# Earlier x sums, a table of Sinkhorn steps and a finer dealing of the last block's L2 in an attention and mixture-of-experts kernel

## The chip, the cores and the metric

The kernel runs on one core of a Trainium2 chip. The metric is the device time of one execution in microseconds (us); the kernel before takes 978.73 us, the median of 6 runs from 977.86 to 979.73.

The core's engines are called as the profile calls them: PE (TensorE, matmuls; PEld is its loading of weights), DVE (VectorE), ACT (ScalarE), POOL (GpSimd) and SP (SyncE, which here only issues DMAs). Each engine takes its own instructions in their order, and semaphores hold an instruction back until what it needs is done.

## The reference

A linear attention with a cosine weighting of the positions makes `x`, and a mixture of 8 experts is applied to all tokens, each expert weighted by a table `P` that Sinkhorn's iteration makes of the gate's logits. The shapes: q, k, v are (8, 8, 576, 64); x is (4608, 512); w1 is (8, 512, 1024), w2 (8, 1024, 512).

```python
k_p, q_p = phi(k, cos_w, sin_w), phi(q, cos_w, sin_w)     # relu, times cos and sin
kv = np.einsum('bhsf,bhsd->bhfd', k_p, v)
z = np.sum(k_p, axis=2)
num = np.einsum('bhsf,bhfd->bhsd', q_p, kv)
den = np.einsum('bhsf,bhf->bhs', q_p, z)[..., None] + 1e-06
x = (num / den)                                           # laid out as tokens x 512
logits = x @ w_gate
P = np.exp(logits - logits.max())
for _ in range(8):
    P /= P.sum(1, keepdims=True) + 1e-09
    P /= P.sum(0, keepdims=True) + 1e-09
    P *= N / E
for e in range(E):
    h = np.maximum(x @ w1[e], 0.0)
    out += P[:, e:e + 1] * (h @ w2[e])
```

## The kernel before

**Two stages.** In the first, blocks 0 to 6, the attention of batch b + 1 is made beside expert 0's two layers of the block of 512 tokens before it. A block has 16 slots (`NS = 2 * FT`): eight for the first layer (`ffn1`, one 128-row slice of the hidden dimension with four matmuls each, then a Relu on ACT into `hT`), eight for the second (`ffn2`, half of a token tile's product over the hidden dimension each, then a copy into `acc`). What the attention does in a slot is written out by hand with `at(block, slot, fn, ...)`. `x`, transposed, lies in one tile `xT`.

In the second stage, blocks 7 and 8 of expert 0 follow (the loop `for j in range(B - 1, NJ)`), then experts 1 to 7 (the loop `for e in range(1, E)`). These multiply 2 x 2 blocks with seven products in place of eight (a Strassen-like scheme), and so need sums of the operands:

- The tokens of an expert are six units (`NU`) of 768 tokens: 384 of the first half of the tokens, 384 of the second. `x_sums(n, ts)` makes unit n's sums S1, S2 and S4 and overwrites a part of `xT`, with four operations of 128 x 768 on DVE, and SP stores the three sums in `x_saved` in DRAM. For later experts `x_again` loads them.
- `w1_steps` gives the four operations that make the sums of one slice of w1 (T2, T3, T4, one in place).
- `group` makes one of four slices of the first layer of a unit: seven products of two matmuls of 384 columns into three PSUM banks X (`h_ps`), Y (`copied_ps`) and Z (`p7_ps` in the program, `p_ps` in the profile). ACT copies X to Y and takes two snapshots u2 and u4 of X, which DVE adds to Z with a clamp (L885). After each product `group` calls `fill()`, seven times in all, in which other work is put between the products. The last product of a group, with its add-and-clamp, is put off (`late`) into the next group.
- `Pair` makes the second layer of two token tiles with seven products P1 to P7 of four matmuls of 256 columns. P1 is copied by ACT into a bank W (L990), and the sums of H that the pair needs are made on DVE (L970); each result is multiplied by a column of `P_tok` and added to `acc` on DVE (L955).

**What the fills hold.** For expert 1's unit 0 the fill is `start_fill`: parts of block 8's second layer, dealt by the generator `dealt` (four parts of two matmuls for each of four token tiles), and steps of Sinkhorn's iteration. From then on it is `pair_fill`: of every four fills three take the next step of the pairs' stream once its place in the stream is due (`slot2`), so that a unit's 28 fills take 21 steps, which are three pairs. `pair_fill` also gates the tiles of `acc` that expert 0 wrote, that is, multiplies them by their column of `P_tok` (`gate`, L1107), as `P_tok` was not known before.

**Sinkhorn's iteration** is the generator `sinkhorn`, with five steps an iteration: (1) row sums and their reciprocal, (2) the table times these, and partial column sums `colp`, (3) up to two of the w1 operations that `tw_steps` holds for the iteration, (4) a matmul of `ones_all` with `colp`, which sums over the partitions, and the remaining w1 operations, (5) a reciprocal and the table times this. `balanced(n)` takes n steps. Eight iterations are 40 steps. The kernel before takes three at slot 1 of block 7, then from slot 5 on one and four in two slots of every five, 23 by the end of block 8, and one in most fills of expert 1's unit 0.

**Order.** While `te`, `ve` and `se` are the wrappers of class `InOrder` (`bound`), the instructions of PE, DVE and ACT stand exactly as written. DVE's is taken away after expert 1's unit 0, ACT's from expert 2 on; the scheduler may then place an instruction as early as its operands allow. Four of the last gatings are so placed in the time of expert 1's first two units.

**Buffers.** The pools of the first stage (`p1`), with `kp_pool` (four buffers `k_p`) and the ones for q and its transposes among them, are closed before the second stage, and its tiles (weights of expert 1, `H`, S1 to S4, T and V) take their place in SBUF, so a write there waits for the last use of what lay there. `H` has two halves that the units take in turn; block 7 writes the half that lies over the `k_p` buffers.

Of the kernel before, what the change touches and what calls it, by code (L numbers as in the profile page):

```python
# [11 lines left out]
F16 = mybir.dt.float16  # L12

AX = mybir.AxisListType
ALU = mybir.AluOpType
# [10 lines left out]
def kernel(  # L26
# [10 lines left out]
    nc = tc.nc  # L37
    P = nc.NUM_PARTITIONS

    B, H, S, D = q.shape  # L40
    E, Dm, F = moe_w1.shape
    N = B * S
# [112 lines left out]
    def ffn2(hT, w, c0, g, y_ps, fts):  # L155

        for ft in fts:
            te.matmul(
                out=y_ps,
                lhsT=hT[:, ft, c0 : c0 + P],  # L160
                rhs=w[1][:, ft, :],
                start=(ft == 0),
                stop=(ft == FT - 1),
            )
        if FT - 1 in fts:

            if g % 2 == 0 or g < (B - 1) * TCH // P:
                se.copy(out=acc(g), in_=y_ps)
            else:
                ve.tensor_copy(out=acc(g), in_=y_ps)  # L170

    def store(g, cols=slice(0, Dm), queues=(nc.sync, nc.sync)):
        for half, queue in enumerate(queues):
            w_ = 2 * g + half
            b, c = w_ // C, w_ % C
            rows = out[b * S : (b + 1) * S].rearrange("(p c) d -> p c d", c=C)
            queue.dma_start(
                out=rows[:, c, cols], in_=acc(g)[half * HP : (half + 1) * HP, cols]
            )

    with ExitStack() as p1:
        ld = p1.enter_context(tc.tile_pool(name="ld", bufs=4))
# [421 lines left out]
        def at(block, slot, fn, *args):  # L604
            todo.setdefault((block, slot), []).append((fn, args))
# [62 lines left out]
        for j in range(B):  # L668
# [82 lines left out]
            if j == 1:  # L751
                for name in "qkv":
                    for half in range(2):
                        at(j, 12, load, b + 2, half, name, True)
            elif j and b + 2 < B:
                for half in range(2):
                    at(j, 11 + half, load, b + 2, half, "qkv", True)
        y_pss = {}
        for j in range(B - 1):
            if j:  # L760
# [34 lines left out]

    NT = N // 2
    TU = 3 * P
    NU = NT // TU  # L800
    KH = KT // 2
    FH = FT // 2
    UG = TU // P
    DH = Dm // 2
    w_next = load_weights(wB, 1)

    H = hB.tile([P, 2, FT, 2 * TU], F16, name="H")
# [12 lines left out]
    Y = ps_k.tile([P, TCH], FP32, name="copied_ps")  # L820
    Z = ps_k.tile([P, TCH], FP32, name="p7_ps")

    def x_part(half, kh, n):
        t0 = half * NT + n * TU
        return xT[:, kh * KH : (kh + 1) * KH, t0 : t0 + TU]

    x_saved = dram.tile([NU, 3, P, KH * TU], F16, name="x_saved")

    def x_tiles():
        return [s2_pool.tile([P, KH, TU], F16, name=name) for name in ("S1", "S2", "S4")]  # L830

    def x_sums(n, ts):

        a11, a12, a21, a22 = (x_part(i, j, n) for i in range(2) for j in range(2))
        s1, s2, s4 = (t[:] for t in ts)
        for out_, in0, in1, op in (
            (s1, a21, a22, ALU.add), (s2, s1, a11, ALU.subtract),
            (s4, a12, s2, ALU.subtract), (a21, a11, a21, ALU.subtract),
        ):
            ve.tensor_tensor(out=out_, in0=in0, in1=in1, op=op)  # L840
            yield
        for i, t in enumerate(ts):
            nc.sync.dma_start(out=x_saved[n, i], in_=t[:].rearrange("p k t -> p (k t)"))

    def x_again(n, ts):
        for i, t in enumerate(ts):
# [8 lines left out]
    def w1_steps(w, i):  # L855

        cols = [slice((j * FH + i) * P, (j * FH + i + 1) * P) for j in range(2)]
        b11, b12 = (w[0][:, 0:KH, c] for c in cols)
        b21, b22 = (w[0][:, KH:KT, c] for c in cols)
        T2, T3, T4 = (t_pool.tile([P, KH, P], F16, name=f"T{k_}_{i}") for k_ in (2, 3, 4))  # L860

        def sub(out, in0, in1, op=ALU.subtract):
            return lambda: ve.tensor_tensor(out=out, in0=in0, in1=in1, op=op)

        steps = [
            sub(T3[:], b22, b12), sub(T2[:], T3[:], b11, ALU.add), sub(b12, b12, b11),
            sub(T4[:], b21, T2[:]),
        ]
        return (b11, b12, b21, b22, T2[:], T3[:], T4[:]), steps
# [216 lines left out]
    def balanced(steps):  # L1086
        for _ in range(steps):
            next(balance, None)

    def dealt(hT, w, tiles, parts):  # L1090

        for i, (c0, g) in enumerate(tiles):
            for part in range(parts):
                ffn2(
                    hT, w, c0, g, rows2[i % 3][:],
                    range(part * FT // parts, (part + 1) * FT // parts),
                )
                yield
# [16 lines left out]

    balance = sinkhorn()

    tws, tw_steps = [], [[] for _ in range(8)]
    for i in range(FH):
        tw, tw_steps[1 + i] = w1_steps(w_next, i)  # L1120
        tws.append(tw)
    xs_first = [x_tiles() for _ in range(2)]
    xs_next = xs_first[0]
    sums_x = x_sums(0, xs_next)
    for j in range(B - 1, NJ):
        hT = next_h()
        tiles = dealt(
            hT, w0, [(ts * P, j * TCH // P + ts) for ts in range(TCH // P)],
            2 if j < NJ - 1 else 4,
        )  # L1130
        for slot in range(NS):
            if slot < FT:
                ffn1(hT, w0, j, [slot])
            elif j < NJ - 1:
                next(tiles)
            else:
                break
            if j == B - 1 and slot == 0:
                gates(B - 1, Z[:])
            if j == B - 1 and slot:  # L1140
                next(sums_x, None)
            if j == NJ - 1:
                if slot == 0:
                    sums_x = x_sums(1, xs_first[1])
                next(sums_x, None)
            since = (j - B + 1) * NS + slot - 5
            if since == -4:
                balanced(3)
            elif since >= 0 and since % 5 < 2:
                balanced((1, 4)[since % 5])  # L1150


    OFFSETS = {"P1": 0, "P2": 3, "P7": 4, "P6": 5, "P4": 8, "P5": 9, "P3": 13}
# [1 line left out]
    OFFSETS_LAST = {"P1": 0, "P2": 3, "P7": 4, "P6": 7, "P5": 8, "P4": 9, "P3": 10}  # L1155
    stream = []
    final = []
    slot2 = -2
    n_pairs = 0

    def add_pairs(hT, e, w, n):
# [13 lines left out]
    def start_fill():  # L1175

        nonlocal k_fill
        if k_fill % 7 in (0, 2, 3, 5):
            next(tiles, None)
        if k_fill % 6 != 1:  # L1180
            balanced(1)
        k_fill += 1

    def pair_fill():
        nonlocal k_fill, slot2
        k_fill += 1
        if k_fill % 4 and stream and stream[0][0] <= slot2:
            _, pair, name = stream.pop(0)
            pair.step(name)
        if (k_fill % 7 == 6 or k_fill % 7 == 4 and k_fill % 4 in (1, 2)) and ungated:  # L1190

            gate(ungated.pop(0))
        slot2 += bool(k_fill % 4)

    mark(Y[:])
    for e in range(1, E):
        if e == 2:
            se = nc.scalar
        w = w_next
        for n in range(NU):  # L1200
            hT = next_h()
            xs = xs_next
            for i in range(FH):
                group(hT, tws[i], xs, n, i, start_fill if e == 1 and n == 0 else pair_fill)
                m = (n + 1) % NU
                if e == 1 and m:

                    if n == 0:
                        xs_next = xs_first[1]
                        continue  # L1210
                    if i == 0:
                        xs_next = x_tiles()
                        sums_x = x_sums(m, xs_next)
                    next(sums_x)
                    if i == FH - 1:
                        next(sums_x, None)
                elif i == 1:
                    xs_next = x_tiles()
                    if not (e == E - 1 and m == 0):
                        x_again(m, xs_next)  # L1220

                if e > 1 and n == 0 and i == 0:
                    tws[FH - 1] = w1_sums(w, FH - 1)
                if e + 1 < E and n == NU - 1:
                    if i:
                        tws[i - 1] = w1_sums(w_next, i - 1)
                    else:
                        w2_first(w_next)
            if e == 1 and n == 0:
                k_fill = 0  # L1230
                for _ in tiles:
                    pass
                for _ in balance:
                    pass
                mark(W2[:])
                w2_first(w)
                for _ in range(2):
                    gate(ungated.pop(0), nc.gpsimd)
                ve = nc.vector
            if n == 0 and e + 1 < E:  # L1240
                w_next = new_weights(wA if e % 2 else wB)
                load_w1(w_next, e + 1, 1)
            if n == 2 and e + 1 < E:
                load_w2(w_next, e + 1, 1)
            add_pairs(hT, e, w, n)
# [36 lines left out]
```

The softmax here doesn't subtract the row's maximum and nothing guards it: scores larger than these inputs give would overflow.

## Time and profile before

| what | us |
|---|---|
| median of 6 runs | 978.73 |
| the profiled execution | 979.73 |
| its span, first to last instruction | 978.0 |
| PE busy | 963.7 |
| DVE busy | 807.3 |
| ACT busy | 563.6 |
| block 6 | about 145 to 164 |
| blocks 7 and 8 | about 164 to 186 |
| expert 1, unit 0 (with block 8's second layer) | about 186 to 208 |
| one unit of a later expert | about 18.4 |
| last group's end to the end | about 961 to 978 |

A row of the timeline has the start, the time from the first start to the last end, the engine, the line and the operation, the tile written and the tiles read, the shape, and how many instructions are merged; in brackets is how long the engine had stood idle and what it then waited for. A line L109 is that of the wrapper `InOrder`, through which most operations go, so that groups are told apart by their tiles; buffer numbers are left out of names, so that `copied_ps` stands for both `copied_ps` and `copied2_ps`, the bank in which the column sums are made.

### The profile page before, as it was taken

What the parts mean: (1) busy time and instruction counts of PE and PEld (TensorE: products, weight loads), DVE (VectorE), ACT (ScalarE), POOL (GpSimd) and SP (SyncE); (2) the same over time, 40 slices, a digit from 0 to 9 for tenths busy, and PEclk for the clock granted to TensorE, in tenths of its full rate; (3) what the DMA queues carried; (4) which work ended last, traced back from release to release, by engine and by line L of the source; (5) the groups of instructions that cost most, each with busy time, mean ns of one, the idle gap of its engine ahead of it and who ended that gap; (6) DMA issues with size and microseconds to landing.
All of it is one profiled execution on the core that took longest, in us unless ns stands there. A gap on an engine that the chain in (4) does not pass through costs nothing.

```text
span 978.0 us, 20236 instructions
## 1 busy us (share of the span) xinstructions
PE 963.7 (99%) x7855; PEld 675.8 (69%) x7855; DVE 807.3 (83%) x1833; ACT 563.6 (58%) x1262; POOL 60.7 (6%) x82
## 2 busy tenths in 40 slices
PE   9999999999999999999999999999999999999997
PEld 6545555457777777777777777777777777777775
DVE  6766775888988888988888888988888888988887
ACT  5756665467776555555555555555555555555551
POOL 6231110010000000000000000000000000000001
PEclk9999999999999999999999999999999999999999
DMA  9999986330103401223103401323103401104435
GB/s 163 182 146 181 152 141 111 68 68 28 48 25 77 84 25 35 64 54 68 39 25 78 83 25 39 62 55 66 40 25 77 84 25 37 38 26 121 127 88 128
DMA packets 80336, 73.54 MB, mean 75 GB/s; under 512 B 33264, under 2 KB 72176, under 8 KB 80240
## 3 DMA queue, kind: packets, MB, share of 16 engines
q0 software_dynamic: 27232, 30.94, 20.3%
q1 hardware_dynamic: 52768, 41.06, 17.5%
q8 instruction: 61, 1.00, 0.4%
q14 instruction: 35, 0.29, 0.1%
q10 hardware_dynamic: 240, 0.26, 0.1%
HBM read 83.12 MB, written 12.98 MB: 98 GB/s over the span
## 4 chain that ended last, share of the span: by engine, by line
PE 89%; DMA 4%; DVE 3%; issue 2%; ACT 1%; POOL 1%; POOLq 0%; ACTq 0%; SPq 0%
PE rows_ps L109 33%; PE h_ps L109 27%; PE p_ps L109 11%; PE copied_ps L109 11%; PE y_ps L109 4%; PE small_ps L109 3%; DMA k_ld<-in_k_dram 1%; DMA w2e<-in_moe_w_dram 1%; DMA w1e<-in_moe_w_dram 1%; DVE P_tok L109 1%; DVE colp L109 0%; POOL q_ld L202 0%; DVE rs L109 0%; DVE acc_hi L955 0%; DVE rr L109 0%
## 5 line engine op out<-in xcount | busy, mean ns | idle before, releaser
L955 DVE SCALAR_TENSOR_TENSOR acc_lo<-rows_ps,P_tok,acc_lo 128x512 f32<-128x512 f32 (+1 forms) x322 | 203.1, 639 | 75.0 <-PE rows_ps L109 74.9
L109 PEld LDWEIGHTS <-H 128*128 128x128 f16 x2080 | 203.1, 98 | 82.5 <-issue 1.2
L891 ACT CAST u<-h_ps 128x384 f16<-128x384 f32 x288 | 137.6, 478 | 131.2 <-PE h_ps L109 131.2
L109 PEld LDWEIGHTS <-w1e 128*128 128x128 f16 x1632 | 157.7, 98 | 67.6 <-issue 5.2
L885 DVE CUSTOM_DVE_ANT_0 H<-p_ps,u 128x384 f16<-128x384 f32 x329 | 180.8, 550 | 6.6 <-PE p_ps L109 6.6
L109 PEld LDWEIGHTS <-hs 128*128 128x128 f16 x1500 | 146.6, 98 | 56.2
L109 PE MATMUL h_ps<-S,w1e 128*128 128x384 f16 x672 | 164.1, 326 | 0.7 <-ACT u L109 0.6
L109 PE MATMUL p_ps<-xT,T 128*128 128x384 f16 x672 | 164.1, 326 | 0.1
L109 PE MATMUL rows_ps<-V,H 128*128 128x256 f16 x1000 | 150.0, 273 | 0.7 <-DVE acc_hi L955 0.7
L109 PE MATMUL rows_ps<-w2e,hs 128*128 128x256 f16 x1000 | 150.0, 273 | 0.0
L109 PE MATMUL h_ps<-xT,w1e 128*128 128x384 f16 (+1 forms) x616 | 148.7, 350 | 0.1
L923 ACT ACTIVATE H<-h_ps 128x384 f16<-128x384 f32 x144 | 70.6, 490 | 95.1 <-PE h_ps L109 95.1
L109 PEld LDWEIGHTS <-T 128*128 128x128 f16 x1008 | 98.4, 98 | 30.1 <-issue 3.6
L109 PE MATMUL rows_ps<-w2e,H 128*128 128x256 f16 (+1 forms) x568 | 92.3, 285 | 0.0
L904 ACT COPY copied_ps<-h_ps 128x384 f32<-128x384 f32 x144 | 67.5, 469 | 35.5 <-PE h_ps L109 35.5
L914 ACT ACTIVATE H<-copied_ps 128x384 f16<-128x384 f32 x144 | 70.8, 492 | 20.4 <-PE copied_ps L109 20.4
L109 PE MATMUL h_ps<-S,T 128*128 128x384 f16 x336 | 81.8, 324 | 0.4 <-ACT copied_ps L109 0.3
L109 PE MATMUL copied_ps<-xT,w1e 128*128 128x384 f16 x336 | 82.1, 326 | 0.0
L109 PE MATMUL copied_ps<-w2e,H 128*128 128x256 f16 x504 | 75.5, 272 | 0.0
L109 PE MATMUL rows_ps<-V,hs 128*128 128x256 f16 x500 | 74.9, 272 | 0.0
L955 DVE SCALAR_TENSOR_TENSOR acc_lo<-copied_ps,P_tok,acc_lo 128x256 f32<-128x256 f32 x126 | 60.0, 476 | 0.6 <-PE copied_ps L109 0.2
L955 DVE SCALAR_TENSOR_TENSOR acc_hi<-rows_ps,P_tok,acc_hi 128x512 f32<-128x512 f32 (+1 forms) x56 | 41.3, 737 | 20.6 <-PE rows_ps L109 19.7
(145 smaller groups left out, 949.9 us busy)
## 6 DMA issues: line engine op xcount, KB each, us to landing
S<-x_saved SPq DMA_DIRECT2D x108, 192.0 KB, 2.4
out_dram<-acc_lo SPq DMA_DIRECT2D x62, 128.0 KB, 2.3
w1e<-in_moe_w_dram POOLq DMA_DIRECT2D x7, 1024.0 KB, 9.1
w2e<-in_moe_w_dram POOLq DMA_DIRECT2D x7, 1024.0 KB, 9.5
q_ld<-in_q_dram POOLq DMA_DIRECT2D x16, 288.0 KB, 6.0
k_ld<-in_k_dram POOLq DMA_DIRECT2D x16, 288.0 KB, 8.2
v_ld<-in_v_dram POOLq DMA_DIRECT2D x16, 288.0 KB, 9.5
x_saved<-S SPq DMA_DIRECT2D x18, 192.0 KB, 1.9
```

The lines of the kernel that those rows point to most:

```text
L109: i = getattr(self.engine, name)(*args, **kwargs)
L885: latest = ve._custom_dve(TENSOR_ADD_SAT, out=out, in0=ps[:, 0:TU], in1=t[:], s0=FP32_MAX, s1=0.0)
L891: se.copy(out=t[:], in_=ps[:, 0:TU])
L904: se.copy(out=Y[:, 0:TU], in_=X[:, 0:TU])
L914: se.activation(out=h11, in_=Y[:, 0:TU], func=AF.Relu)
L923: se.activation(out=h12, in_=X[:, 0:TU], func=AF.Relu)
L955: ve.scalar_tensor_tensor(out=a, in0=rows, scalar=P_tok[:, g, self.e : self.e + 1], in1=a, op0=ALU.mult, op1=ALU.add,)
```

## The change

- The first two units' x sums are made by `x_sums_early` in block 6, at slots 5 and 9, in `k_p` buffers, and stored in `x_saved`. The second stage loads them with `x_again` into `xs_first`. In the kernel before they were made in blocks 7 and 8, one operation a slot. `x_part`, `x_saved` and `x_sums` move up in the text for this.
- Sinkhorn's steps follow two tables: 28 steps in blocks 7 and 8, at slots 1, 4, 8, 13, 17 and 22 counted from block 7's start, and 12 in the fills of `start_fill`. The w1 operations are dealt to the iterations as 2, 3, 4, 3 and 4, beginning with the first, where each of iterations 1 to 4 had four.
- Block 8's second layer is dealt in eight parts for a tile, of one matmul each: one part a fill and twice two. The two parts that are left, and the copy of tile 35, come in the first `pair_fill`, behind `mark` (a matmul that writes the bank W2); they came before it. The dealt tiles take the three PSUM banks `rows2` in another turn.
- Block 7's two odd tiles are copied by ACT instead of DVE.
- The pairs' stream starts one place earlier (`slot2 = -1`).

```diff
-            if g % 2 == 0 or g < (B - 1) * TCH // P:
+            if g % 2 == 0 or g < B * TCH // P:
                 se.copy(out=acc(g), in_=y_ps)
             else:
                 ve.tensor_copy(out=acc(g), in_=y_ps)
...
+    x_saved = dram.tile([NU, 3, P, KH * TU], F16, name="x_saved")
+
+    def x_sums(n, ts):
+
+        a11, a12, a21, a22 = (x_part(i, j, n) for i in range(2) for j in range(2))
+        s1, s2, s4 = ts
+        for out_, in0, in1, op in (
+            (s1, a21, a22, ALU.add), (s2, s1, a11, ALU.subtract),
+            (s4, a12, s2, ALU.subtract), (a21, a11, a21, ALU.subtract),
+        ):
+            ve.tensor_tensor(out=out_, in0=in0, in1=in1, op=op)
+            yield
+        for i, t in enumerate(ts):
+            nc.sync.dma_start(out=x_saved[n, i], in_=t.rearrange("p k t -> p (k t)"))
...
+        def x_sums_early(n):
+            ts = [kp_pool.tile([P, C, 2, D], F16, name="k_p") for _ in range(3)]
+            for _ in x_sums(n, [
+                t[:].rearrange("p c a d -> p (c a d)")[:, 0 : KH * TU].rearrange(
+                    "p (k t) -> p k t", k=KH
+                ) for t in ts
+            ]):
+                pass
+
+        for n in range(2):
+            at(B - 2, (5, 9)[n], x_sums_early, n)
...
-                    hT, w, c0, g, rows2[i % 3][:],
+                    hT, w, c0, g, rows2[(i + 2) % 3][:],
...
-    tws, tw_steps = [], [[] for _ in range(8)]
+    tws, steps_left = [], []
     for i in range(FH):
-        tw, tw_steps[1 + i] = w1_steps(w_next, i)
+        tw, steps = w1_steps(w_next, i)
         tws.append(tw)
+        steps_left += steps
+    tw_steps = [[steps_left.pop(0) for _ in range(n)] for n in (2, 3, 4, 3, 4, 0, 0, 0)]
     xs_first = [x_tiles() for _ in range(2)]
     xs_next = xs_first[0]
-    sums_x = x_sums(0, xs_next)
+    for n in range(2):
+        x_again(n, xs_first[n])
...
-            2 if j < NJ - 1 else 4,
+            2 if j < NJ - 1 else 8,
...
-            if j == B - 1 and slot:
-                next(sums_x, None)
-            if j == NJ - 1:
-                if slot == 0:
-                    sums_x = x_sums(1, xs_first[1])
-                next(sums_x, None)
-            since = (j - B + 1) * NS + slot - 5
-            if since == -4:
-                balanced(3)
-            elif since >= 0 and since % 5 < 2:
-                balanced((1, 4)[since % 5])
+            balanced({1: 3, 4: 5, 8: 5, 13: 5, 17: 5, 22: 5}.get((j - B + 1) * NS + slot, 0))
...
-    slot2 = -2
+    slot2 = -1
...
     def start_fill():
 
         nonlocal k_fill
-        if k_fill % 7 in (0, 2, 3, 5):
+        for _ in range(1 + (k_fill % 14 == 1)):
             next(tiles, None)
-        if k_fill % 6 != 1:
-            balanced(1)
+        balanced({3: 1, 4: 1, 6: 1, 8: 2, 12: 1, 13: 1, 15: 1, 17: 2, 21: 1, 22: 1}.get(k_fill, 0))
         k_fill += 1
...
         k_fill += 1
+        for _ in range(2):
+            next(tiles, None)
         if k_fill % 4 and stream and stream[0][0] <= slot2:
...
             if e == 1 and n == 0:
                 k_fill = 0
-                for _ in tiles:
-                    pass
                 for _ in balance:
                     pass
```

More of the change, by code (lines that the diff above doesn't have):

```diff
@@ L179, in store, with x_part @@
             )
+    NT = N // 2
+    TU = 3 * P
+    NU = NT // TU
+    KH = KT // 2
+    FH = FT // 2
+    UG = TU // P
+    DH = Dm // 2
+    def x_part(half, kh, n):
+        t0 = half * NT + n * TU
+        return xT[:, kh * KH : (kh + 1) * KH, t0 : t0 + TU]
+    x_saved = dram.tile([NU, 3, P, KH * TU], F16, name="x_saved")
[10 more added lines that the diff above has]
+            nc.sync.dma_start(out=x_saved[n, i], in_=t.rearrange("p k t -> p (k t)"))
     with ExitStack() as p1:
@@ L788 @@
     hs_pool = ctx.enter_context(tc.tile_pool(name="hs_pool", bufs=2))
[L798 to L804, printed above, removed]
     w_next = load_weights(wB, 1)
@@ L821 @@
     Z = ps_k.tile([P, TCH], FP32, name="p7_ps")
[L823 to L827, printed above, removed]
     def x_tiles():
         return [s2_pool.tile([P, KH, TU], F16, name=name) for name in ("S1", "S2", "S4")]
[L832 to L843, printed above, removed]
     def x_again(n, ts):
@@ L1212 @@
                         xs_next = x_tiles()
-                        sums_x = x_sums(m, xs_next)
+                        sums_x = x_sums(m, [t[:] for t in xs_next])
                     next(sums_x)
```

## The prediction, made before the changed kernel was run

> **What bounds the kernel now.** The page's first line first: it names the engine that can be waited for.
>
> ```profile
> PE 963.7 (99%) x7855; PEld 675.8 (69%) x7855; DVE 807.3 (83%) x1833; ACT 563.6 (58%) x1262; POOL 60.7 (6%) x82
> ```
>
> TensorE (PE) sets the time, and its work is the same after the change, so only its idle time can be won. Where that lies is told by busy time by stretch (columns: stretch, length, then busy us of each engine):
>
> ```profile
> 164.00:186.00 22.00, 21.97 (x124) 10.44 (x123) 17.32 (x45) 10.46 (x19) 0.00 (x0) 1.00 0.13 45
> 186.00:208.00 22.00, 18.70 (x100) 9.46 (x99) 16.91 (x42) 12.60 (x27) 4.54 (x4) 1.00 0.33 63
> 208.00:216.00 8.00, 7.42 (x53) 4.93 (x51) 7.93 (x17) 6.39 (x15) 0.29 (x1) 1.00 1.03 167
> 216.00:420.00 204.00, 203.82 (x1550) 151.21 (x1549) 178.56 (x406) 128.65 (x284) 2.39 (x3) 1.00 0.21 50
> 420.00:800.00 380.00, 379.82 (x2903) 283.59 (x2902) 324.27 (x727) 211.09 (x477) 5.79 (x7) 1.00 0.25 53
> ```
>
> PE idles 22.00 - 18.70 = 3.30 us in expert 1's first unit (186 to 208), 0.58 in the next 8 us, almost nowhere else until the last pairs. The waits name whom it waited for:
>
> ```profile
> PE copied_ps L109 <- DVE colp L109: 3.0, 4, 1.2
> ```
>
> These are Sinkhorn's column sums: a product of `ones_all` with `colp`, four times late. The PE timeline gives their true size, which "busy" understates, because a matmul's listed end lies beyond the start of the next: two 512 column matmuls are listed at 0.59 us, but the next group starts 0.43 later (189.34 to 189.77); two of 384 columns take 0.325.
>
> ```profile
> 186.99 0.59 PE L109 MATMUL rows_ps<-w2e,H 128*128 128x512 f16 x2
> 188.78 0.39 PE L109 MATMUL copied_ps<-colp,ones_all 128*128 128x8 f32 x2 [1.19 <-DVE colp L109]
> ...
> 189.34 0.59 PE L109 MATMUL rows_ps<-w2e,H 128*128 128x512 f16 x2
> 189.77 0.49 PE L109 MATMUL copied_ps<-xT,w1e 128*128 128x384 f16 x2
> ...
> 191.61 0.49 PE L109 MATMUL h_ps<-S,w1e 128*128 128x384 f16 x2
> 192.41 0.39 PE L109 MATMUL copied_ps<-colp,ones_all 128*128 128x8 f32 x2 [0.31 <-DVE colp L109]
> ...
> 195.91 0.59 PE L109 MATMUL rows_ps<-w2e,H 128*128 128x512 f16 x2
> 197.24 0.39 PE L109 MATMUL copied_ps<-colp,ones_all 128*128 128x8 f32 x2 [0.74 <-DVE colp L109]
> ...
> 200.44 0.49 PE L109 MATMUL h_ps<-S,w1e 128*128 128x384 f16 x2
> 201.67 0.39 PE L109 MATMUL copied_ps<-colp,ones_all 128*128 128x8 f32 x2 [0.74 <-DVE colp L109]
> ```
>
> Start to start the four waits are 188.78 - 187.42 = 1.36, 192.41 - 191.94 = 0.47, 197.24 - 196.34 = 0.90 and 201.67 - 200.77 = 0.90: 3.63 us. Two smaller ones (178.92 and 183.62; twenty 512 column matmuls end 4.31 after their start) are 0.20 and 0.15. VectorE (DVE) is late because the x sums of unit 1 stand among the Sinkhorn steps:
>
> ```profile
> 185.07 0.55 DVE L109 TENSOR_TENSOR xT<-xT 128x768 f16<-128x768 f16 x1
> ...
> 185.94 0.20 DVE L109 RECIPROCAL t<-copied_ps 128x8 f32<-128x8 f32 x1
> ...
> 188.06 0.67 DVE L109 TENSOR_REDUCE colp<-P_tok 128x8 f32<-128x288 f32 x1
> ```
>
> From `t` to the end of `colp` an iteration takes 188.06 + 0.67 - 185.94 = 2.79 us. The other idle time is ScalarE's (ACT): snapshots of a product stand behind gatings (L1107, 0.72 each):
>
> ```profile
> 208.43 0.46 ACT L109 COPY copied_ps<-h_ps 128x384 f32<-128x384 f32 x1
> 208.80 0.72 ACT L1107 ACTIVATE acc_hi<-acc_hi,P_tok 128x512 f32<-128x512 f32 x1
> 209.47 0.48 ACT L109 CAST u<-h_ps 128x384 f16<-128x384 f32 x1
> 209.90 0.36 ACT L109 COPY copied_ps<-rows_ps 128x256 f32<-128x256 f32 x1
> ```
>
> Start to start PE loses 0.21 (204.28), 0.44 (207.31), 0.45 (208.94) and 0.46 (211.14) to it: 1.56 us.
>
> **What the Trainium skill says.** "Perfetto Trace Analysis", Tensor Engine Instruction: "ACT/DVE/GPSIMD are strict FIFO". The trace agrees: the snapshot at 209.47 started only when the gating before it let go. So a walk along each engine's order is the right method. "DMA: Bandwidth & Descriptors", Anatomy of one DMA, puts a fixed cost of about 2 us on a DMA, most of it the write receipt; here a 192 KB store of x sums landed 1.8 to 1.9 us after its issue. The same page, Issuing engines are not separate DMA queues: transfers of all issuers run on the same 16 DMA engines; here loads of the sums took 2.2 to 3.9, with weights in flight for some.
>
> **The change part by part.** I lay the changed order of instructions along this profile's times.
>
> *x sums in block 6.* Eight 128x768 operations (0.47 us start to start) leave the Sinkhorn stretch, 3.7 us. In block 6 the first four follow `hl` (ends 154.4), the next four the numerators that end at 159.1; DVE idled 3.19 and 3.12 us there, and each four take 1.9. The second four need the stores of the first (issued 155.0 to 156.2; by 160.1 at the worst seen 3.9, while they reach those buffers at 159.5 and 160.0). Price: nothing, else some tenths that end before the numerators of 162.25. On SP the order is three stores, three loads, three stores, three loads. The first loads wait for their stores and for a numerator of 157.7; so unit 1's stores go out at 160.6 to 161.8 and land at 162.5 to 165.7. The buffers lie where block 7's first half of `H` is written, so the first Relu of block 7 (165.20 before) now waits for them. PE has 0.55 us of slack there. Taken: nothing; bound: from 0 to 2.5 us if landings take 5 to 6. The loads are wanted at 187, late by nothing.
>
> *Sinkhorn's table, five column sums in blocks 7 and 8.* PE reaches them at 168.95, 172.55, 177.0, 180.6 and 185.1 (slots of 0.865, 0.14 a sum). `colp` is ready at 168.0; then each time 0.33 (from the sum to `t`) plus 2.79 after the sum before: 172.1, 175.7, 180.1, 183.7. No wait; smallest margin 0.4. The w1 sums stand where DVE has idle time. The sixth, at fill 3, is ready at 188.3, and PE arrives at 188.4 (from 186.07: `mark` 0.22, three products of 0.325, five parts of 0.215, and 0.06 of waiting for `copied_ps`): margin 0.1. The seventh and eighth: 192.9 against 193.4, and 198.0 against 198.6, with the two add-and-clamp operations (0.55) and one copy (0.68) between counted. Both copies of block 7 that move to ACT (0.58) stand in its idle time (3.00 and 2.44 before). So 3.63 + 0.35 = 3.98 us go, 0.1 taken back.
>
> *L2 product by product.* 32 parts of one matmul instead of 16 of two: the same matmuls. The last two go behind `mark`, so the copy of tile 35 comes later, and a gating in ACT's order waits for that copy: DVE has the x sums' S4, the w2 subtraction (0.60) and an add-and-clamp ahead of it. Walk from the end of the last product of unit 1 (time 0): copy 1.23 to 1.91; gating from 1.97; then the copy of the first pair's product (0.33), then the snapshot, ready 3.38. PE wants it at 2.37: 1.06 lost. Before that, a snapshot behind a gating: 0.29. Together 1.35 against 1.56: 0.2 won.
>
> *Pairs one slot earlier.* The steps stand at the same fills; only which step changes. In the five units of expert 1 with gatings a wait of 0.16 (217.26, 235.88, ...) for `copied_ps` behind a gating behind a pair's copy goes, since that copy now comes two products earlier: 5 x 0.16 = 0.8. In every unit the first pair's copy now stands ahead of a snapshot: copy done 2.20, snapshot 2.20 to 2.68, wanted at 2.77 (from the unit's start): slack 0.04 after 0.05 for the semaphore. Price: 0; bound 0 to 0.2 a unit. Last pairs: one step fewer runs after the last group, and its wait of 0.16 (961.36) goes.
>
> Sum: 3.98 - 0.1 + 0.2 + 0.8 + 0.16 = 5.0 us. The two thin margins (0.1 and 0.04) and the Relu will not all hold; I take 0.5 for them, an estimate: 4.5 us. The profiled execution took 979.73 with a span of 978.0, 1.0 above the median of 978.73; the span goes to 973.5, the median to 974.2.
>
> **Rivals.**
> - Block 7 waits for the stores. For it: the new wait, behind SP's order and weights in flight until 163. Against: 192 KB landed in 1.9. At 2.5 us: 976.7.
> - DVE stays late, so that the column sums still wait and only the pairs' and half the sums' gain is left, 1 us: 977.7. For it: margins of 0.1 to 0.6. Against: 3.7 us of DVE work have left.
> - Slower: in each of the 41 units with pairs the first pair's copy delays the snapshot. Its place is ACT's order at the second fill, its price 0.2 us a unit, 41 x 0.2 = 8.2, so 974.2 + 8.2 = 982.4. It decides from 4.5 / 41 = 0.11 a unit. For it: slack 0.04. Against: PE waits for snapshots nowhere from 300 to 940 now, with slacks of 0.05 beside `copied_ps`.
>
> **How the numbers follow.** Forecast 0.62, stores 0.15, DVE late 0.11, copies 0.12. A difference of 0.2%, 2 us, is about what this measurement can tell from none. Faster: nearly all of the first and half of the second, 0.70; slower 0.12; the rest, 0.18, no change. Range: 972.9 (all 5.0, and 0.8 of the two waits of 0.51 among the last pairs at 964.93 and 968.49, for which nothing is counted) to 978.7 (DVE late, or the copies' delay at 0.1 a unit); the likeliest alone 973.4 to 975.6.
>
> **What would show it.** Right: no wait of PE for `colp`; a PE idle time near 1 us some 5 us after expert 1's first unit; that unit 4 us shorter; units of 18.4 us after 300 as now. Wrong: a wait of PE for ACT's `H` at 165 to 167 (stores); PE waits for `u` in every unit (copies); `colp` still in PE's waits (DVE).

## The result and the profile after

The changed kernel takes 983.59 us (median of 33 runs, 981.56 to 989.09) against 978.87 us for the kernel before (70 runs, 977.18 to 985.06). The ratio is 1.0049 with an interval of 1.0041 to 1.0058: slower by half a per cent, where 974.2 us was forecast. The profiled execution of the changed kernel took 985.25 us with a span of 983.5, so it is 1.7 us longer than the median; that of the kernel before had a span of 978.0.

The first line of the page says that PE does the same work and stands still longer (98% of a longer span).

```profile
PE 962.8 (98%) x7855; PEld 676.1 (69%) x7855; DVE 817.6 (83%) x1831; ACT 566.0 (58%) x1264; POOL 60.7 (6%) x82
```

Busy time by stretch (stretch, length, busy us of PE, PEld, DVE, ACT and POOL, then the granted PE clock, the DMA share and GB/s) says where:

```profile
164.00:186.00 22.00, 18.16 (x92) 8.32 (x91) 12.79 (x35) 7.13 (x14) 0.00 (x0) 0.84 0.29 89
186.00:208.00 22.00, 21.52 (x120) 11.61 (x119) 16.77 (x42) 14.42 (x29) 0.95 (x2) 1.00 0.29 49
208.00:216.00 8.00, 6.81 (x45) 4.18 (x44) 7.80 (x16) 6.93 (x15) 3.89 (x3) 1.00 0.57 114
216.00:420.00 204.00, 202.87 (x1543) 150.56 (x1541) 179.98 (x405) 128.72 (x284) 2.39 (x3) 1.00 0.22 50
420.00:800.00 380.00, 377.80 (x2891) 282.33 (x2890) 328.16 (x723) 210.99 (x475) 5.79 (x7) 1.00 0.25 53
```

From 164 to 186 PE idled 0.03 us before and 3.84 now, and its clock fell to 0.84: block 7. From 186 to 208 the idle time fell from 3.30 to 0.48: the column sums. From 420 to 800 it rose from 0.18 to 2.20: something that comes back in every expert.

Busy time hides a part of each wait, so I added up, over the trace, what each PE step from start to start has beyond the usual step of its kind of product (0.162 us for 384 columns, 0.109 for 256, 0.2155 for 512):

| stretch, us | before | after | difference |
|---|---|---|---|
| up to 160 | 40.4 | 39.7 | -0.7, waits for DMAs; this stretch differs from trace to trace (about 38 to 42 in this study) |
| 160 to 180: block 7 | 1.3 | 8.1 | +6.8 |
| 180 to 220: block 8, expert 1's first units | 6.6 | 2.8 | -3.8 |
| 220 to 312: rest of expert 1 | 1.8 | 2.3 | +0.4 |
| 312 to 956: experts 2 to 7 | 3.4 | 6.2 | +2.8 |
| after 956 | 2.8 | 2.6 | -0.2 |

The sum is +5.3 us, the spans differ by 5.5. PE's waits (us in total, times, longest) carry three new rows, the one for `u` has grown from 0.6, and the one for `colp` is gone:

```profile
PE p_ps L109 <- DVE H L898: 3.5, 7, 0.6
PE h_ps L109 <- ACT H L109: 2.8, 1, 2.8
PE h_ps L109 <- ACT u L109: 1.2, 2, 0.9
PE h_ps L109 <- DVE xT L109: 1.1, 2, 0.7
```

**Block 7.** PE's timeline, and below it DVE's and ACT's for the same time:

```profile
163.53 0.59 PE L109 MATMUL h_ps<-xT,w1e 128*128 128x512 f16 x2
164.83 0.38 PE L109 MATMUL h_ps<-xT,w1e 128*128 128x512 f16 x1 [0.71 <-DVE xT L109]
165.56 0.38 PE L109 MATMUL h_ps<-xT,w1e 128*128 128x512 f16 x1 [0.35 <-DVE xT L109]
...
166.34 1.02 PE L109 MATMUL h_ps<-xT,w1e 128*128 128x512 f16 x4
170.14 5.28 PE L109 MATMUL h_ps<-xT,w1e 128*128 128x512 f16 x12 [2.77 <-ACT H L109]
```

```profile
158.44 0.55 DVE L109 TENSOR_TENSOR k_p<-xT 128x768 f16<-128x768 f16 x1
162.02 0.56 DVE L109 TENSOR_TENSOR k_p<-k_p,xT 128x768 f16<-128x768 f16 x1 [3.03 <-DMA x_saved<-k_p]
163.29 0.56 DVE L109 TENSOR_TENSOR k_p<-xT,k_p 128x768 f16<-128x768 f16 x1 [0.71 <-DMA x_saved<-k_p]
163.76 0.55 DVE L109 TENSOR_TENSOR xT<-xT 128x768 f16<-128x768 f16 x1
164.23 1.54 DVE L109 TENSOR_TENSOR xT<-small_ps,rb 128x384 f16<-128x384 f32 x4
```

```profile
169.49 0.60 ACT L109 ACTIVATE H<-h_ps 128x512 f16<-128x512 f32 x1 [5.18 <-DMA x_saved<-k_p]
```

The reader is to see one chain. In block 6 DVE starts unit 1's sums at 158.44, but the second sum goes into a buffer that unit 0's store still reads, so DVE stands 3.03 and 0.71 us. Behind it in DVE's order are the last numerators (164.23, four operations), which block 7's first products need: PE loses 0.87 and 0.51, start to start. Unit 1's stores then go out only at 164.9 to 165.9, and the first Relu of block 7, at 165.20 before, runs at 169.49, when they have landed (the last at 168.95; ACT then still passes a row of semaphore waits about 0.08 us apart): PE loses 2.94. The last line of PE's timeline shows a second cost. Twelve products of 512 columns are listed at 5.28 us; they start 0.427 us apart, not 0.2155: half clock for 5 us, another 2.6 us lost.

All of it hangs on the stores. The trace view of the stores' line (time from issue to landing) in the changed kernel, and below it that of the stores in the kernel before:

```profile
DMA to landing us min/median/max: 3.0/5.4/9.1
```

```profile
DMA to landing us min/median/max: 1.8/1.9/1.9
```

Unit 0's three stores took 7.7, 8.3 and 9.1 us (issued 154.27 to 155.46, landed 161.93 to 164.51). Expert 1's w1 and w2, 1 MB each, were on their way from 149.1 to 166.0.

### The profile page after: what moved, and what is told of

The parts are those of the page before. It is cut to its first block, busy times and chain, and to the rows that moved or that the text cites. A ratio compares the mean times of both kernels' runs of the same rounds, so it can differ in the third digit from the quotient of the medians.

```text
span 983.5 us, 20240 instructions
## 1 busy us (share of the span) xinstructions
PE 962.8 (98%) x7855; PEld 676.1 (69%) x7855; DVE 817.6 (83%) x1831; ACT 566.0 (58%) x1264; POOL 60.7 (6%) x82
## 4 chain that ended last, share of the span: by engine, by line
PE 84%; DVE 7%; DMA 5%; issue 3%; POOL 1%; ACT 0%; DVEq 0%; ACTq 0%; POOLq 0%; SPq 0%
PE rows_ps L109 31%; PE h_ps L109 25%; PE p_ps L109 10%; PE copied_ps L109 10%; PE y_ps L109 4%; PE small_ps L109 2%; DVE H L898 1%; DMA k_ld<-in_k_dram 1%; DMA w2e<-in_moe_w_dram 1%; DMA w1e<-in_moe_w_dram 1%; DVE hs L983 1%; DVE acc_lo L968 1%; DVE acc_hi L968 1%; DMA acc_hi<-q_p 1%; DVE S L203 1%
## 5 line engine op out<-in xcount | busy, mean ns | idle before, releaser
L898 DVE CUSTOM_DVE_ANT_0 H<-p_ps,u 128x384 f16<-128x384 f32 x329 | 181.3, 551 | 59.2 <-PE p_ps L109 53.8
L109 PE MATMUL h_ps<-xT,w1e 128*128 128x384 f16 (+1 forms) x616 | 152.1, 356 | 3.9 <-ACT H L109 2.8
L109 PE MATMUL rows_ps<-w2e,H 128*128 128x256 f16 (+1 forms) x568 | 94.4, 285 | 0.0
L1003 ACT COPY copied_ps<-rows_ps 128x256 f32<-128x256 f32 x111 | 39.6, 357 | 30.1 <-PE rows_ps L109 30.1
```

The costliest lines, as they stand in the source:

```text
L109: i = getattr(self.engine, name)(*args, **kwargs)
L898: latest = ve._custom_dve(TENSOR_ADD_SAT, out=out, in0=ps[:, 0:TU], in1=t[:], s0=FP32_MAX, s1=0.0)
L1003: se.copy(out=self.W, in_=self.U)
```

## Experiments

Theory A: the loss is the stores of the x sums, slow because of the weights in flight beside them, on which block 7 waits; what follows in PE's clock comes from that wait; and a smaller loss in every expert comes from the pairs' new slot. Theory B, the prediction's slower rival: the loss lies in the units, where the pair's copy delays a snapshot. Every run below was timed beside the kernel before (medians of 978.50 to 978.75 us).

### The other half of H for block 7 (after_halves)

```diff
-        return H[:, turns_h % 2]
+        return H[:, (turns_h + 1) % 2]
```

> The changed kernel, but block 7 writes the other half of H, which does not lie over the buffers of the x sums until its last slots. Theory A (block 7 stands still because its first Relu may not overwrite sums that are still being stored, and PE then runs at half clock): the wait of 2.94 us and the half clock of 2.6 us go, the numerators stay late by 1.39 us: 983.6 - 5.5 = 978.1. Theory B (the loss lies in the units of the experts, and the wait at block 7 is absorbed elsewhere): within 0.5 us of 983.6.

Measured: 982.9 us, ratio 1.0038 (1.0025 to 1.005). In its trace the Relu still waits for `x_saved<-k_p`, and PE still loses 2.84 us there. So block 7 does not wait for the bytes that it overwrites. In the built program the first write to `H`, in this kernel as in the changed one, waits for all six stores: all pools of the first stage are closed before `H` is made, and its first write waits for the DMAs that last used them. This run tells nothing of theory B either.

### w2's load behind the stores (after_w2_behind)

```diff
+            stored.append(
                 nc.sync.dma_start(out=x_saved[n, i], in_=t.rearrange("p k t -> p (k t)"))
+            )
...
-        load_w2(w, e, 1)
+        load_w2(w, e, 1, stored[-1])     # its DMA waits: after(stored[-1], i)
```

> The changed kernel, but expert 1's w2 load waits until the last store of x sums has landed. Theory A with its cause (the stores took 7.7 to 9.1 us instead of 1.9 because 2 MB of weights were in flight beside them): stores land in 2 to 4 us, VectorE is not stopped before unit 1's sums, block 7 starts without a wait: 983.6 - 7 = 976.6. If the stores are slow for another reason (SP's order, their place): 983.6, and the same 8 us landings.

Measured: 978.09 us, ratio 0.9991 (0.9983 to 0.9998): 5.5 us less than the changed kernel. The stretch of block 7, PE's waits and the stores' times (in the order of these three views):

```profile
164.00:186.00 22.00, 22.00 (x128) 11.02 (x126) 16.49 (x46) 11.98 (x21) 0.89 (x1) 1.00 0.43 78
```

```profile
PE p_ps L109 <- DVE H L904: 3.5, 7, 0.6
...
PE h_ps L109 <- ACT u L109: 1.2, 2, 0.9
```

```profile
DMA to landing us min/median/max: 3.5/3.8/4.2
```

PE does not idle in block 7 at all, its clock is 1.00, and the waits for `H` of ACT and for `xT` are gone. Unit 0's three stores now take 4.0 to 4.2 us in place of 7.7 to 9.1, with w1 still in flight beside them. Nothing else was moved, neither SP's order nor the stores' place, so the weights in flight made them slow. The expected 976.6 was 1.5 too low: it was reckoned from the profiled execution of the changed kernel, which is 1.7 above the median.

### The pairs at their old slot (after_slot2)

```diff
-    slot2 = -1
+    slot2 = -2
```

> The changed kernel with the pairs back at their old slot (slot2 = -2). Theory A: the wait of 0.71 us for an add-and-clamp behind three w2 operations, once in each of 6 experts, goes back to 0.26: 6 x 0.45 = 2.7, and some 0.3 in expert 1: 980.6. The rival of the prediction (a copy ahead of a snapshot costs 0.2 us in each of 41 units): 983.6 - 8.2 = 975.4. If the pairs' place is without effect: 983.6.

Measured: 980.63 us, ratio 1.0021 (1.0011 to 1.0032): 3.0 us less than the changed kernel, as theory A has it. Experts 2 to 7 lose 3.1 us beyond the usual steps in place of 6.2. Where it comes from stands in DVE's timeline of the changed kernel in expert 2's first unit, with PE's below:

```profile
322.03 0.68 DVE L1000 TENSOR_TENSOR V<-w2e 128x1024 f16<-128x1024 f16 x1
...
323.49 0.68 DVE L1001 TENSOR_TENSOR V<-V,w2e 128x1024 f16<-128x1024 f16 x1
324.09 0.42 DVE L983 TENSOR_TENSOR hs<-H 128x512 f16<-128x512 f16 x1
324.42 0.68 DVE L1010 TENSOR_TENSOR V<-w2e,V 128x1024 f16<-128x1024 f16 x1
...
325.70 0.74 DVE L968 SCALAR_TENSOR_TENSOR acc_hi<-rows_ps,P_tok,acc_hi 128x512 f32<-128x512 f32 x1
326.36 0.41 DVE L983 TENSOR_TENSOR hs<-H,hs 128x512 f16<-128x512 f16 x1
326.69 0.55 DVE L898 CUSTOM_DVE_ANT_0 H<-p_ps,u 128x384 f16<-128x384 f32 x1
```

```profile
324.73 0.49 PE L109 MATMUL p_ps<-xT,T 128*128 128x384 f16 x2
...
326.25 0.49 PE L109 MATMUL h_ps<-xT,w1e 128*128 128x384 f16 x2
327.29 0.48 PE L109 MATMUL p_ps<-xT,T 128*128 128x384 f16 x2 [0.55 <-DVE H L898]
```

The first pair of an expert makes three differences of w2, 0.68 us each. With the pairs one slot earlier the third (L1010) stands ahead of the add-and-clamp (L898) that empties Z, whose product starts at 324.73. It runs at 326.69, and PE, which wants Z again at 326.58, starts at 327.29: 0.71 us, in each of six experts. At the old slot (after_slot2) the order on DVE is add-and-clamp first, third difference after:

```profile
324.38 0.54 DVE L898 CUSTOM_DVE_ANT_0 H<-p_ps,u 128x384 f16<-128x384 f32 x1
324.85 0.68 DVE L1010 TENSOR_TENSOR V<-w2e,V 128x1024 f16<-128x1024 f16 x1
```

The other units of an expert have no such wait, and PE waits for no `u` in experts 2 to 7 of the changed kernel (its two large waits for `u` are at 209.14 and 213.16, and the five of 0.2 us in expert 1 were there before): theory B falls.

### The early sums alone, in the kernel before (before_early)

Edit: only `x_sums_early` and its two places in block 6, with the loads of the saved sums; the table of slots, the L2 and the pairs stay as before.

> The kernel before, with the first two units' x sums made in block 6 as the change makes them and nothing else of the change. Theory A: block 7 loses 7.3 us as in the changed kernel, and the column sums win up to 4 us because 8 VectorE operations leave their stretch: 978.9 + 7.3 - 4 = 982.2, up to 986.2. Theory B: 975 to 979.

Measured: 982.53 us, ratio 1.004 (1.0024 to 1.0056), within the range of theory A. Block 7 shows the same waits; but here the products after the wait of 2.89 us ran at full speed (sixteen in 3.61 us):

```profile
165.95 0.38 PE L109 MATMUL h_ps<-xT,w1e 128*128 128x512 f16 x1 [0.54 <-DVE xT L109]
166.68 0.38 PE L109 MATMUL h_ps<-xT,w1e 128*128 128x512 f16 x1 [0.35 <-DVE xT L109]
...
171.37 3.61 PE L109 MATMUL h_ps<-xT,w1e 128*128 128x512 f16 x16 [2.89 <-ACT H L109]
```

So the half clock does not follow in every execution. Waits for `colp` fell from 4 to 2 (by PE's list of waits from 3.0 to 1.5 us): early sums help the column sums, as the change meant them to, and cost more than they bring.

### PE kept busy while it waits (after_filled)

```diff
+            if j == B - 1 and slot == 1:
+                for _ in range(12):
+                    mark(W2[:])
```

> The changed kernel with 12 idle products of 512 columns (12 x 0.216 = 2.6 us, into a bank that nobody reads) put where PE waits 2.9 us for the Relu in block 7. If the half clock that follows the wait (0.427 instead of 0.216 us a product, 1.7 to 2.6 us lost in four of five profiles so far) comes from PE standing still, it goes, the wait itself stays: about 983.6 - 1.7 = 981.9, and every product of block 7 at 0.216. If it comes from something else (the DMAs, a disturbance), the products after the wait still take 0.427 and the time is 983.6.

Measured: 982.4 us, ratio 1.0034 (1.0022 to 1.0045). The products behind the wait ran at 0.2155 again:

```profile
166.39 2.75 PE L109 MATMUL copied_ps<-xT 128*128 128x512 f16 x12
169.40 2.75 PE L109 MATMUL h_ps<-xT,w1e 128*128 128x512 f16 x12 [0.25 <-ACT H L109]
```

The mean clock of its six runs is 1.000 in five and 0.999 in one; of 34 executions of the changed kernel 31 are at 0.998 or below. So the half clock is what PE's standing still leaves behind. In the changed kernel it is worth 1.2 us in the median (the two intervals overlap a little). The Trainium skill, "TensorE: Matmul & The Clock Gate", Part 1, says that the clock halves after an idle window of about 3.4 us and that the window runs free of the kernel. A window that runs free fits a cost that comes in some executions (2.6 us in the changed kernel's profile, about 1.7 in those of after_slot2 and after_halves) and not in others (none in before_early), and a clock record that stands at one half for 3.41 us in these two traces and for 6.83, twice that, in the changed kernel's. The idle window itself does not fit: waits of 2.3 to 3.0 us, less than a window, were enough here, and in the 3.41 us before the clock turned PE had still been busy for 0.8 to 1.6 us.

### x sums back in blocks 7 and 8 (after_no_early)

Edit: `x_sums_early` gone, the sums made slot by slot in blocks 7 and 8 as before; the rest of the change kept.

> The changed kernel with the first two units' x sums made in blocks 7 and 8 again, as in the kernel before; table of slots, product by product and pairs as in the change. Theory A: block 7 starts without a wait (7 us less), and the 8 VectorE operations of 0.47 us that are back in the Sinkhorn stretch delay column sums by 0 to 3.7 us: 976.5 to 980. If the column sums wait nowhere even so, the early sums were needed for nothing: 976.5 to 977. If block 7 still stands still: 983.6.

Measured: 978.33 us, ratio 1.0001 (0.999 to 1.0012). No wait in block 7; two column sums wait again, at 173.36 (0.31) and 190.03 (0.74), 1.3 us in all by start to start against 4.6 before (the 3.98 of the prediction, and 0.1 for each of six late sums, whose own two products then take longer). So the rest of the change, with the sums where they were, takes away 3.3 us of waiting for `colp`, the early sums another 1.3. For that they cost more: without them the kernel is 5.3 us faster. Even with the stores repaired (978.09 in after_w2_behind) they bring no gain over 978.33 that these intervals can tell.

### Both repairs (w2_slot2)

Edit: w2's load behind the stores and `slot2 = -2` together.

> The changed kernel with expert 1's w2 load behind the stores and with the pairs at their old slot. The two effects lie in different places and should add: 978.1 - 2.9 = 975.2. If one had hidden the other: 977 or more.

Measured: 975.36 us, ratio 0.9964 (0.9951 to 0.9976). The two gains (5.5 and 3.0) nearly add, and the kernel is faster than the one before.

### The last gatings on GpSimd, or in five more places (w2_slot2_pool, w2_slot2_gates)

What is left at the start of expert 1's second unit are PE's waits for snapshots, 0.42, 0.22 and 0.99 us. Two edits, each on top of w2_slot2:

```diff
-            gate(ungated.pop(0))
+            gate(ungated.pop(0), nc.gpsimd if se is nc.scalar else None)
```

> As the run above, and the last four gatings, which the scheduler puts to the front of ScalarE's order at the start of expert 1's second unit, are made by GpSimd (1.56 us each in the profile, beside other work). If PE's waits for snapshots there (0.42, 0.22 and 0.99 us) come from these gatings, they go: 975.2 - 1.5 = 973.7. If they come from VectorE's late copy of the last tile alone, less than 0.3 goes: 975.

```diff
-        if (k_fill % 7 == 6 or k_fill % 7 == 4 and k_fill % 4 in (1, 2)) and ungated:
+        if (k_fill % 7 == 6 or k_fill % 7 == 4 and k_fill % 4 < 3) and ungated:
```

> Expert 1's w2 load behind the stores, pairs at their old slot, and five more places for gatings in expert 1, so that none is left for expert 2 to be put to the front of ScalarE's order. If PE's waits for snapshots at the start of the second unit (0.42, 0.22 and 0.99 us) come from those four gatings: 975.4 - 1.6 + (0 to 0.2 for each of the five units) = 973.8 to 974.8. If they come from VectorE's late copy: 975.4 or a little more.

Measured: 976.3 us, ratio 0.9973 (0.996 to 0.9987), and 975.48 us, ratio 0.9961 (0.9949 to 0.9973): neither is faster than 975.36. With GpSimd all but 0.26 us of these waits went, so the gatings did make them; with five more places 0.42 and 0.22 went and 0.86 stayed. Others came in both (add-and-clamps of 0.21 and 0.41 us with the five places). With the gatings on GpSimd two of DVE's three w2 differences took 1.09 and 1.11 us in place of 0.68. DVE's timeline, and GpSimd's below it:

```profile
207.47 0.68 DVE L1006 TENSOR_TENSOR V<-w2e 128x1024 f16<-128x1024 f16 x1
...
208.40 1.09 DVE L1007 TENSOR_TENSOR V<-V,w2e 128x1024 f16<-128x1024 f16 x1
...
211.78 1.11 DVE L1016 TENSOR_TENSOR V<-w2e,V 128x1024 f16<-128x1024 f16 x1
```

```profile
203.22 4.69 POOL L1128 TENSOR_SCALAR acc_lo<-acc_lo,P_tok 128x512 f32<-128x512 f32 x3 [13.92 <-DVE P_tok L109]
207.89 1.94 POOL L1128 TENSOR_SCALAR acc_hi<-acc_hi,P_tok 128x512 f32<-128x512 f32 x1
209.81 1.79 POOL L1128 TENSOR_SCALAR acc_lo<-acc_lo,P_tok 128x512 f32<-128x512 f32 x1
211.55 0.95 POOL L133 DMA_DIRECT2D w2e<-in_moe_w_dram  x1
212.54 1.78 POOL L1128 TENSOR_SCALAR acc_hi<-acc_hi,P_tok 128x512 f32<-128x512 f32 x1
```

and PE waited 1.43 us for an add-and-clamp. "GPSIMD Engine Reference" of the Trainium skill (its table of specifications) has it that GpSimd shares its SBUF interfaces with VectorE and contends with instructions of two SBUF inputs; these differences are such, and GpSimd's own gating took 1.94 us beside the first slow one in place of 1.56. But the trace agrees only in part: the first difference (207.47), with two such inputs and beside the same work, kept its 0.68, and the second slow one (211.78) lies for the most part beside a DMA that GpSimd issues. Which of them collide is not settled here. With five more places, each of four later units lost 0.2 us. In the profile of the first of these runs block 7 also waited 0.90 us for `H`: with w1 still in flight the stores' margin is thin.

### H as two tiles, unit 1's sums in q_p's buffers (after_split, split_slot2_gates)

Block 7 writes the lower of the two tiles. split_slot2_gates has `slot2 = -2` and the five places for gatings as well.

```diff
-            ts = [kp_pool.tile([P, C, 2, D], F16, name="k_p") for _ in range(3)]
+            ts = [
+                kp_pool.tile([P, C, 2, D], F16, name="k_p") if n == 0
+                else qp_pool.tile([P, C, 2, D], F16, name="q_p")
+                for _ in range(3)
+            ]
...
-    H = hB.tile([P, 2, FT, 2 * TU], F16, name="H")
+    H = [hB.tile([P, FT, 2 * TU], F16, name=f"H{i}") for i in range(2)]
...
-        return H[:, turns_h % 2]
+        return H[(turns_h + 1) % 2]
```

> The changed kernel with H as two tiles, block 7 in the lower one, and unit 1's x sums in the buffers of q_p instead of k_p; the weights are loaded as in the change. The run with the halves swapped left the wait as it was, since H was one tile and its first write waited for everything that lay anywhere under it. Theory A: now no store lies under the first Relu but those of unit 0, which land at about 164; VectorE does not wait for a buffer; PE has no wait in block 7 although the stores still take 8 us: 983.6 - 5.5 = 978.1, or 977. If the slow DMAs themselves, and not the buffers, are what block 7 suffers from: 983.

Measured: 981.3 us, ratio 1.0022 (1.0008 to 1.0036): a gain of 2.3 us where 5.5 was expected. DVE no longer stands, and the numerators are in time: PE's waits for `xT` are gone. But the Relu still comes after the last store.

```profile
166.08 0.58 ACT L109 COPY acc_lo<-y_ps 128x512 f32<-128x512 f32 x1 [1.86 <-PE y_ps L109]
169.79 0.60 ACT L109 ACTIVATE H<-h_ps 128x512 f16<-128x512 f32 x1 [3.12 <-DMA w2e<-in_moe_w_dram]
```

The releaser named is a load that landed at 169.76; the built program's Relu has no wait for that load, but for all six stores, of which the last landed at 169.61, though unit 1's lie outside this tile of `H`. The trace agrees: ACT's semaphore waits before the Relu let go at 166.80, 168.15, 169.11 and 169.63, each 0.02 us after a store's landing, the last three of them unit 1's. So neither place that was tried for `H` and the sums frees block 7; stores that land earlier do. Unit 1's stores took 6.8 to 7.1 us here: w1 had just landed when they were issued, but w2 and unit 0's stores were still in flight. The six runs at a mean clock of 1.000 took 979.5 to 980.6 us, the six at 0.996 to 0.998 took 982.0 to 984.6: the half clock again, though not all of this difference need come from block 7.

> H as two tiles and unit 1's x sums in q_p's buffers, pairs at their old slot, five more places for gatings; the weights loaded as in the change. If the three repairs are independent: 983.6 - 5.5 - 2.9 - 1.2 = 974.0.

Measured: 978.33 us, ratio 0.9991 (0.9983 to 0.9999), 4.3 above the expectation, with the same wait for the stores (2.4 us) and half clock behind it.

### The L2 dealt in parts of two products again (w2_slot2_tiles)

```diff
-            2 if j < NJ - 1 else 8,
+            2 if j < NJ - 1 else 4,
...
-        for _ in range(1 + (k_fill % 14 == 1)):
+        if k_fill % 7 in (0, 2, 3, 5):
             next(tiles, None)
...
-        for _ in range(2):
-            next(tiles, None)
...
+                for _ in tiles:
+                    pass
```

> As the run with the w2 load behind the stores and the old slot of the pairs, but with the last block's L2 dealt in parts of two products again, all done before expert 1's first unit ends. Prediction's step (product by product wins 0.2 us): 975.6. By the traces, where dealing by product goes with waits of 0.65 + 0.42 + 0.22 + 0.99 = 2.3 us against 1.56 before: 974.7.

Measured: 974.53 us, ratio 0.9954 (0.9942 to 0.9965), the fastest version seen. Its interval overlaps that of w2_slot2, so that the dealing itself makes a difference is not shown by the times; over 180 to 220 us PE loses 2.9 us against 3.1.

## Why the prediction was wrong

- **"x sums in block 6 ... Price: nothing", "bound: from 0 to 2.5".** This is the step that failed first. The wait was named (the first Relu behind the stores, and SP's order), though its reason, that the buffers lie under `H`, is not what counts (after_halves, after_split). The size was wrong, and with it the sign of the whole. The store was priced at 1.8 to 1.9 us, from stores that ran with no weights in flight, or 3.9 at worst, from loads of 192 KB. (The fixed 2 us that the prediction takes from "DMA: Bandwidth & Descriptors", Anatomy of one DMA, are given there for DMAs that GpSimd issues; these stores are SP's, and their price came from the trace.) Unit 0's took 7.7 to 9.1 us, because 2 MB of weights were in flight beside them, which the profile of before showed to last until 164. The late landing was paid three times: DVE's second four sums (expected to reach the buffers when they were free), the numerators behind them, and unit 1's stores, issued at 164.9 in place of 160.6. The price was 6.8 us in the profile and 5.5 in the median, half clock included; no step of the prediction counted what a wait does to PE's clock.
- **"Sinkhorn's table": right.** 3.98 us were to go and 0.1 to come back; no column sum waits for `colp` in the changed kernel, and 4.6 went, as the late sums' own products had also been longer. Block 8 and expert 1's first units gained 3.8 us, with what the next point took back.
- **"L2 product by product ... 1.35 against 1.56: 0.2 won": half right.** The loss at the start of unit 1, forecast as 1.06, measured 1.09. The one before it was forecast at 0.29 and measured 0.42, and a third was missed, 0.65 at 198.50: a product waits there for `copied_ps`, whose copy stands in ACT's order behind the copy of a finished tile. In all 2.2 us against 1.56, so by the profiles the step costs some tenths; the times do not show it (w2_slot2_tiles).
- **"Pairs one slot earlier": wrong.** In expert 1 the five waits of 0.16 went, as forecast; waits for add-and-clamps of 0.23 (three times) and 0.38 came in their place, so that a gain of 0.8 became a loss of 0.4. In each later expert the wait of 0.71 came, 2.8 us in all (4.3, less smaller waits that went) where nothing was counted. "Only which step changes" was tried against ACT's order (the copy and its slack of 0.04, which held) and not against DVE's, where P1 of an expert's first pair brings two w2 differences and P7 a third.
- **The rivals.** "Block 7 waits for the stores" was the right one, at 2.5 us in place of 5.5 and with a chance of 0.15. "DVE stays late" did not come. The slower rival came out near the measured time (982.4) by luck: its sign, a wait of PE for `u` in every unit, is absent.

Forecast and result lie 9.4 us apart: 5.5 for block 7, 3.0 for the pairs at their new slot (by the runs), and about 1 us of gain that was counted for the pairs.

## What to carry to other kernels

Price a DMA by what is in flight when it is issued, not by the same DMA at a quiet time: here a store of 192 KB took 1.9 us with no weights in flight, 4 beside w1 (1 MB), and 7 to 9 where w2 (another 1 MB) was under way as well. Before putting a store at the end of a stage, list who waits for it; in this program the first write after a change of pools waited for the stores out of the old ones, wherever these lay. When a step of a written order moves, walk it past every engine that it issues on, and walk its rare forms (the first of an expert, the last of all) as well as the common one.

## What was not expected of the hardware

A wait of PE of 2.3 to 3.0 us left the half clock behind it, for about 3 to 5 us, in five profiles, and one of 3.05 us left none in a sixth; filled with idle products the same wait left none. Beside gatings of 1.56 us a tile on GpSimd, or a DMA that it issues, two VectorE operations on SBUF took 1.1 us in place of 0.68, while a third kept its 0.68.
